# A transformer block with its backward pass on one core: a centred start, a reordered W2 stage, later h1 stores and one reordered FFN pair

## Chip, cores, metric

One core of one Trainium2 chip. The metric is the device time of one execution in microseconds (us), lower is better.

## The reference

Forward and backward of one block: layernorm, linear attention with 32 heads of 20, layernorm, gated FFN. x is 2048 x 640, the FFN is 1728 wide, all in bf16. What the change touches is the forward half:

```python
def _A_ref(x, wqkv, wo):                     # x is already layernormed
    q, k, v = ...                            # x @ wqkv, 32 heads
    phi = lambda t: jnp.where(t > 0, t + 1, jnp.exp(t)) + 1e-6
    pq, pk = phi(q), phi(k)
    kv = jnp.einsum("bhsd,bhse->bhde", pk, v)
    z = jnp.einsum("bhsd->bhd", pk)
    ...                                      # (pq kv) / (pq z) @ wo
h  = x + _A_ref(_layernorm(x), wqkv, wo)
h2 = h + _B_ref(_layernorm(h), w_gate, w_up, w_down)     # (silu(g) * u) @ w_down
# returned: h2 and the gradients for x and the five weights
```

## The kernel before

Sixteen token tiles of 128 rows. In the start, each tile is normalised on VectorE, transposed on TensorE (`ps_t`), copied by ScalarE (`xnT`) and multiplied with the k and q weights (`ps_kq`); exp and relu are ScalarE's, the rest of phi VectorE's.

```python
    def ln1(t):
        nc.vector.tensor_scalar(out=xn[:, t, :], in0=x_tm[...], scalar1=mv1[:, t, 0:1],
                                scalar2=rstd1[:, t:t + 1], op0=ALU.subtract, op1=ALU.mult)
        ...  # 5 transposes into ps_t, nc.scalar.copy into xnT
    # ... (cut)
        warm(42); ln1_stats(0); ln1(0); warm(10)
        act = kq_mm(0, 0); ln1(1); act()
        ln1_stats(2); kq_mm(1, 0)(); kq_mm(0, 1)()
        for t in range(1, ST):
            if t + 1 < ST: ln1(t + 1)
            if t == 2: kq_phi(0)
            if t > 1: kq_mm(t, 0)()
            if t + 2 < ST: ln1_stats(t + 2)
            # ... (cut)
            kq_mm(t, 1)()
            if t > 1: kq_phi(t - 1)
```

Then come z, Y = xn^T pk (`ps_y`), KV, and the W2 stage. `dm(1)` is an independent piece of FFN backward, ten products and a ScalarE copy, used as filler.

```python
        for t in range(0, 12, 4):
            normalise(t)                       # VectorE, about 8.3 us
            if t < 8: tr_pqs(t)                # four DMA transposes on SP
        for t in range(3): load_xr(t)
        # ... KV products and their VectorE masks (cut)
        dm(1)
        for i in range(DT):
            ps = mm("ps_w2t")
            mm_heads(ps, ...)
            nc.scalar.copy(out=half(W2T[:, i, :]), in_=row(ps))
            nc.sync.dma_start_transpose(out=W2[...], in_=W2T[:, i, :])
        tr_pqs(8); normalise(12); tr_pqs(12)
        dm(4)
        for t in range(ST + 2):
            if t < ST:
                xr = xrs.pop(t)
                ps = mm("ps_a"); mm_row(ps, ...)                       # pqsT x W2
                nc.vector.tensor_tensor(out=half(xr[:]), in0=row(ps), in1=half(xr[:]), op=ALU.add)
                nc.scalar.dma_start(out=scr_h1_v[:, t, :], in_=xr[:])  # the h1 store
                # ... statistics (cut)
                dm(1)
            if t > 0: load_xr(t + 2)
            u = t - 2
            # ... hn(u) on VectorE, its transpose on SP (cut)
```

Four FFN groups follow (`pg`, `pu`, seven VectorE multiplications and sums a tile pair, then `ps_dw`, the weight gradient), and from `ps_dhn` on the backward of attention, which the change touches in one VectorE line (`tk`).

The names in short: pqs is pq divided by its normaliser; ps_a is the output of attention, xr are the rows of x to which it is added, and the sum is h1; hn is h1 normalised; pg and pu are the gate and up products of the FFN. A name with ps_ is a tile in PSUM, where TensorE's products land; the program uses these buffers in turn, so a product may have to wait until the copy out of its buffer has ended. "Before" and "after" are the first two traces.

Of the kernel before, what the change touches and what calls it, by code (L numbers as in the profile page):

```python
# [10 lines left out]
ALU = mybir.AluOpType  # L11
# [4 lines left out]
P = 128  # L16
# [4 lines left out]
def kernel(  # L21
# [8 lines left out]
    nc = tc.nc  # L30
# [36 lines left out]
    def row(ps):  # L67
        return ps[:, :, :320]
# [35 lines left out]

    def mm_row(ps, lhs, rhs, n, start=True, stop=True, by_k=False):

        steps = [(ci, k) for ci in range(2) for k in range(n)]
        if by_k:
            steps.sort(key=lambda x: x[1])
        for ci, k in steps:  # L110
            nc.tensor.matmul(ps[:, ci, :320], lhsT=lhs(k), rhs=rhs(k, *NCH[ci]),  # L111
                             start=(start and k == 0), stop=(stop and k == n - 1))

# [84 lines left out]

    nc.sync.dma_start(out=x_tm[0][:, 0, 0:320], in_=x_v[:, 0, 0:320])
    nc.scalar.dma_start(out=x_tm[0][:, 0, 320:640], in_=x_v[:, 0, 320:640])  # L200
    load_x(nc.scalar, 1, 2)
    w_k = A_wqkv[:, D:2 * D].rearrange("(k p) n -> p k n", p=P)
    nc.sync.dma_start(out=wqk[:, 0:3, D:2 * D], in_=w_k[:, 0:3, :])
    nc.sync.dma_start(out=wqk[:, 3:5, D:2 * D], in_=w_k[:, 3:5, :])
# [6 lines left out]
    def load_2():  # L211
        yield load_x(nc.sync, 2, 3)
        yield nc.sync.dma_start(out=wqk[:, :, 0:D], in_=A_wqkv[:, 0:D].rearrange("(k p) n -> p k n", p=P))
        yield load_x(nc.sync, 3, 4)

    def load_3():
# [43 lines left out]
    ers = {}  # L260

    def ln1_stats(t):
        st = ln_stats(x_tm[t // 8][:, t % 8, :], mv1[:, t, :])
        if t == 0:
            wait_for(st, load_2())
        ln_rstd(mv1[:, t:t + 1, :], rstd1, t, 1, nc.vector if t < 2 else nc.gpsimd)

    def ln1(t):
        nc.vector.tensor_scalar(out=xn[:, t, :], in0=x_tm[t // 8][:, t % 8, :], scalar1=mv1[:, t, 0:1],
                                scalar2=rstd1[:, t:t + 1], op0=ALU.subtract, op1=ALU.mult)  # L270
        tp = psum.tile([P, D], BF16, name="ps_t", tag="mm")
        for kt in range(DT):
            nc.tensor.transpose(tp[:, kt * P:(kt + 1) * P], xn[:, t, kt * P:(kt + 1) * P], ident[:])
        tpv = tp[:].rearrange("p (k c) -> p k c", c=P)
        if t == 0:
            ln1_stats(1)
            wait_for(nc.scalar.copy(out=xnT[:, t, 0:3], in_=tpv[:, 0:3]), load_3())
            nc.scalar.copy(out=xnT[:, t, 3:5], in_=tpv[:, 3:5])
        else:
            nc.scalar.copy(out=xnT[:, t], in_=tpv)  # L280

    def kq_mm(t, which):
        dst, w0 = ((pk, D), (pqa, 0))[which]
        ps = mm("ps_kq")
        mm_row(ps, lambda k: xnT[:, t, k, :], lambda k, n0, n1: wqk[:, k, w0 + n0:w0 + n1], DT, by_k=(t == 0))

        def act():
            e = fw("phi_e")
            r = fw("phi_r")
            nc.scalar.activation(out=e[:, :, :320], in_=row(ps), func=ACT.Exp)  # L290
            nc.scalar.activation(out=r[:, :, :320], in_=row(ps), func=ACT.Relu)
            ers.setdefault(t, []).append((dst, e, r))

        return act
# [14 lines left out]
    with tc.manual_schedule(engines={EngineType.PE, EngineType.DVE, EngineType.Activation}):  # L309
# [6 lines left out]

        warm(42)
        ln1_stats(0)
        ln1(0)
        warm(10)  # L320
        act = kq_mm(0, 0)
        ln1(1)
        act()
        ln1_stats(2)
        kq_mm(1, 0)()
        kq_mm(0, 1)()
        for t in range(1, ST):
            if t + 1 < ST:
                ln1(t + 1)
            if t == 2:  # L330
                kq_phi(0)
            if t > 1:
                kq_mm(t, 0)()
            if t + 2 < ST:
                ln1_stats(t + 2)
            if t == 1:
                kq_phi(0, last=False)
            kq_mm(t, 1)()
            if t > 1:
                kq_phi(t - 1)  # L340
        kq_phi(ST - 1)

# [91 lines left out]
    with tc.manual_schedule(engines={EngineType.PE, EngineType.DVE, EngineType.SP}):  # L434
# [15 lines left out]
        dm(1)  # L450
        for t in range(0, 12, 4):
            normalise(t)
            if t < 8:
                tr_pqs(t)
        for t in range(3):
# [15 lines left out]
        dm(1)  # L471
        for i in range(DT):
            ps = mm("ps_w2t")
            mm_heads(ps, lambda j: wo6[:, j, i * P:(i + 1) * P], lambda j, a, b: KVT[:, j, a:b])
            nc.scalar.copy(out=half(W2T[:, i, :]), in_=row(ps))
            nc.sync.dma_start_transpose(out=W2[:, :, i * P:(i + 1) * P], in_=W2T[:, i, :])
        tr_pqs(8)
        normalise(12)
        tr_pqs(12)
        dm(4)  # L480

# [3 lines left out]
        for t in range(ST + 2):  # L485
            if t < ST:
# [3 lines left out]
                nc.vector.tensor_tensor(out=half(xr[:]), in0=row(ps), in1=half(xr[:]), op=ALU.add)  # L490
                nc.scalar.dma_start(out=scr_h1_v[:, t, :], in_=xr[:])
                mv = small.tile([P, 4, 2], FP32, name="mv2", tag="mv2")
# [11 lines left out]
            if u == 2:  # L504
                nc.sync.dma_start(out=mat_v(scr_W2T), in_=W2T)
            h1, mv = h1s.pop(u)
            nc.vector.tensor_scalar(out=hn[:, u, :], in0=h1[:], scalar1=mv[:, 0, 0:1],
                                    scalar2=rstd2[:, u:u + 1], op0=ALU.subtract, op1=ALU.mult)
# [3 lines left out]
    with tc.manual_schedule(engines={EngineType.SP}):  # L512
# [13 lines left out]
        for g in range(4):  # L526
# [4 lines left out]
            for t in range(0, ST, 2):  # L531
# [27 lines left out]
                nc.scalar.copy(out=u, in_=pu[:, :, :w])  # L559
                a = fw("a")[:, :, :w]  # L560

                nc.vector.tensor_tensor(out=m, in0=m, in1=dg, op=ALU.mult)  # L562
                nc.vector.tensor_tensor(out=a, in0=u, in1=dmv, op=ALU.mult)
                nc.vector.tensor_tensor(out=nsg, in0=nsg, in1=m, op=ALU.mult)
                nc.vector.tensor_tensor(out=du, in0=m, in1=dmv, op=ALU.mult)
                nc.vector.tensor_tensor(out=nsg, in0=nsg, in1=dg, op=ALU.add)
                nc.vector.tensor_tensor(out=m, in0=m, in1=u, op=ALU.mult)  # L567
                nc.vector.tensor_tensor(out=dg, in0=a, in1=nsg, op=ALU.mult)
                for c in range(2):
# [146 lines left out]
    with tc.manual_schedule(engines={EngineType.SP, EngineType.DVE}):  # L716
# [65 lines left out]
        WK2 = wvk[:, 1]  # L782
        for i in range(DT):
            ps = mm("ps_wk2")
            mm_heads(ps, lambda j: wqkvT[:, 10 + j, i * P:(i + 1) * P], lambda j, a, b: dKVT[:, j, a:b])
            nc.scalar.copy(out=half(WK2[:, i, :]), in_=row(ps))
            nc.sync.dma_start_transpose(out=WV2[:, :, i * P:(i + 1) * P], in_=WK2[:, i, :])
        ps = mm("ps_dzb")
        mm_row(ps, lambda k: ones[:], lambda k, n0, n1: dzE[k][:, n0:n1], 2)
# [29 lines left out]
        for t in range(ST + LAG):  # L819
            if t in (2, 3):  # L820
                dwqk(0, t + 1, t + 2)
            if t < ST:
# [6 lines left out]
                mm_row(ps, lambda i: xnT_r[:, t, i, :], lambda i, n0, n1: WK2[:, i, n0:n1], DT)  # L829
                nc.vector.tensor_tensor(out=half(tk[:]), in0=row(ps), in1=half(dzb[:]), op=ALU.add)  # L830
                nc.vector.tensor_tensor(out=dk[:, t, :], in0=tk[:], in1=pkr[:], op=ALU.mult)
# [118 lines left out]
```

## Time and profile before

| kernel before | us |
|---|---|
| median of the first runs (823.25 to 825.19) | 823.6 |
| the profiled one of these | 825.2 |
| TensorE busy in it | 815.3 of a span of 823.3 |

The prediction below shows the waits and the chain. A line of the timeline gives start, duration, engine, line, operation, tile, sizes, count; in brackets idle time before and what ended it. Kernel before, W2 stage:

```profile
91.45 2.20 PE L130 MATMUL ps_w2t<-yk,wvo 128*128 128x120 bf16 x35
...
91.65 0.91 ACT L377 CAST dm<-ps_dm 128x896 bf16<-128x896 f32 x1 [2.79 <-PE ps_dm L363]
92.45 3.09 ACT L475 CAST wvo<-ps_w2t 128x640 bf16<-128x640 f32 x5
...
93.80 2.43 PE L363 MATMUL ps_dm<-wdT,dh2T 128*128 128x448 bf16 x12
```

Thirty-five small products take TensorE from 91.45 to 93.80, 2.35 us for five tiles. ScalarE needs 0.91 and 3.09 us for the copies that empty those PSUM tiles, one after the other. TensorE is shown busy, yet its starts show that it is held to ScalarE's pace: the products of the fourth tile start at 92.61 and those of the fifth at 93.20, each right after a copy has ended (92.55 and 93.15).

### The profile page before, as it was taken

Reading aid. Unit: us, or ns where it says so; the run is one execution under the profiler, and the core shown is the slowest. Engines: PE = TensorE matmul, PEld = TensorE weight load, DVE = VectorE, ACT = ScalarE, POOL = GpSimd, SP = SyncE. Lnnn points to the kernel's source line nnn. Section 1 sums busy time; section 2 is a strip of 40 time slices with the busy share of each in tenths; the row PEclk is TensorE's granted clock in tenths of the full one; section 3 lists DMA queues with packets and bytes.
Section 4 is the critical chain, followed back from the end, with each engine's and each line's share of the span. In section 5 each row is a group of like instructions: output and inputs, shape, how many; then the busy total and the mean of one; then the engine's idle time right before and its main releaser. Section 6 shows DMA issues by size and latency. Waiting matters only on the chain.

```text
span 823.3 us, 14095 instructions
## 1 busy us (share of the span) xinstructions
PE 815.3 (99%) x5549; PEld 522.8 (63%) x5549; DVE 444.0 (54%) x875; ACT 291.3 (35%) x412; POOL 187.2 (23%) x343
## 2 busy tenths in 40 slices
PE   8999999999999999999999999999999999999998
PEld 6766656555555555555556677777776777777776
DVE  6978767791077018810660147787884366632222
ACT  6982422670084125500741122322322133322101
POOL 2330022322312231221126301211220112112330
PEclk9999999999999999999999999999999999999999
DMA  9993589999658898893498937978599989899942
GB/s 300 191 355 88 137 190 262 284 231 201 163 104 202 190 215 204 195 264 86 99 252 185 286 72 218 232 195 175 115 241 160 177 147 183 170 191 266 268 135 73
DMA packets 278369, 158.53 MB, mean 193 GB/s; under 512 B 235036, under 2 KB 264925, under 8 KB 278304
## 3 DMA queue, kind: packets, MB, share of 16 engines
q1 hardware_dynamic: 251600, 81.96, 53.6%
q0 software_dynamic: 17744, 64.45, 25.1%
q10 hardware_dynamic: 8960, 11.24, 4.2%
q8 instruction: 43, 0.70, 0.4%
q14 instruction: 22, 0.18, 0.1%
HBM read 47.60 MB, written 53.66 MB: 123 GB/s over the span
## 4 chain that ended last, share of the span: by engine, by line
PE 85%; DVE 8%; DMA 3%; ACT 1%; SPq 1%; issue 1%; POOL 0%; ACTq 0%; DVEq 0%
PE ps_dw L607 20%; PE ps_dhn L111 14%; PE ps_dxn L852 8%; PE ps_o L907 7%; PE ps_dwqk L111 5%; PE ps_kq L111 4%; PE pg L535 4%; PE pu L540 4%; PE ps_dm L363 3%; PE ps_y L111 3%; PE ps_dk L111 3%; PE ps_gt L658 3%; PE ps_dp L111 3%; PE pdm L363 2%; DMA xr<-in_A_x_dram 1%; DVE m_s L562 1%
## 5 line engine op out<-in xcount | busy, mean ns | idle before, releaser
L111 PE MATMUL ps_dhn<-wgT,cols 128*128 128x320 bf16 x864 | 119.5, 299 | 0.0
L607 PE MATMUL ps_dw<-dd,hn 128*128 128x448 bf16 (+1 forms) x640 | 118.8, 346 | 0.0
L111 PEld LDWEIGHTS <-cols 128*128 128x128 bf16 x864 | 84.5, 98 | 32.9
L607 PEld LDWEIGHTS <-hn 128*128 128x128 bf16 x640 | 62.6, 98 | 54.2
L609 DVE CAST dwev<-ps_dw 128x896 bf16<-128x896 f32 (+3 forms) x12 | 10.9, 908 | 124.0 <-PE ps_dw L607 124.0
L609 ACT CAST dwev<-ps_dw 128x896 bf16<-128x896 f32 (+1 forms) x20 | 17.6, 878 | 158.5 <-PE ps_dw L607 158.5
L572 POOL DMA_DIRECT2D scr_dT<-stg x64 | 34.7, 542 | 168.4 <-DMA stg<-dd 162.2
L149 DVE CUSTOM_DVE_ANT_0 lb_a<-lb_dy,hn 128x640 bf16<-128x640 bf16 x32 | 26.4, 826 | 75.4 <-ACT lb_dy L147 75.4
L540 PE MATMUL pu<-wgu,hnT 128*128 128x448 bf16 (+1 forms) x320 | 63.6, 346 | 0.0
L535 PE MATMUL pg<-wgu,hnT 128*128 128x448 bf16 (+1 forms) x320 | 63.6, 346 | 0.0
L907 PE MATMUL ps_o<-wd,mT 128*128 128x320 bf16 (+2 forms) x462 | 62.8, 295 | 0.0
L607 PE MATMUL ps_dw<-m_s,dh 128*128 128x448 bf16 (+1 forms) x320 | 60.7, 346 | 0.6 <-DVE m_s L567 0.6
L852 PEld LDWEIGHTS <-ring 128*128 128x128 bf16 x480 | 46.9, 98 | 18.3
L907 PEld LDWEIGHTS <-mT 128*128 128x128 bf16 x462 | 44.0, 98 | 16.2 <-issue 0.3
L852 PE MATMUL ps_dxn<-wqkvT,ring 128*128 128x320 bf16 x320 | 51.3, 299 | 0.0
L607 PEld LDWEIGHTS <-dh 128*128 128x128 bf16 x320 | 31.3, 98 | 28.0 <-issue 1.1
L540 PEld LDWEIGHTS <-hnT 128*128 128x128 bf16 x320 | 31.3, 98 | 27.1
L535 PEld LDWEIGHTS <-hnT 128*128 128x128 bf16 x320 | 31.3, 98 | 27.1
L363 PEld LDWEIGHTS <-dh2T 128*128 128x128 bf16 x320 | 31.2, 98 | 26.6 <-issue 1.5
L363 PE MATMUL ps_dm<-wdT,dh2T 128*128 128x448 bf16 (+1 forms) x240 | 46.7, 344 | 1.2 <-ACT dm L377 1.0
L111 PE MATMUL ps_kq<-wqk,xnT 128*128 128x320 bf16 x320 | 46.1, 300 | 0.9 <-ACT xnT L280 0.8
L147 ACT ACTIVATE lb_dy<-ps_dhn,rstd 128x640 bf16<-128x640 f32 x16 | 12.7, 793 | 87.6 <-PE ps_dhn L111 87.6
(160 smaller groups left out, 1276.4 us busy)
## 6 DMA issues: line engine op xcount, KB each, us to landing
scr_dT<-stg POOLq DMA_DIRECT2D x48, 224.0 KB, 3.1
cols<-scr_dT POOLq DMA_DIRECT2D x6, 1728.0 KB, 8.4
scr_m<-m_s POOLq DMA_DIRECT2D x12, 448.0 KB, 4.4
cols<-scr_dT ACTq DMA_DIRECT2D x2, 1728.0 KB, 8.3
out_dram<-dwev POOLq DMA_DIRECT2D x30, 112.0 KB, 2.2
scr_dT<-stg POOLq DMA_DIRECT2D x16, 192.0 KB, 2.6
scr_pk<-pk SPq DMA_DIRECT2D x4, 640.0 KB, 7.6
scr_pq<-pqa SPq DMA_DIRECT2D x4, 640.0 KB, 7.9
```

The source lines that it names most:

```text
L111: nc.tensor.matmul(ps[:, ci, :320], lhsT=lhs(k), rhs=rhs(k, *NCH[ci]), start=(start and k == 0), stop=(stop and k == n - 1))
L147: nc.scalar.activation(out=half(dy[:]), in_=row(ps), func=ACT.Copy, scale=rstd_col, accum_out=sums[:, 0:1])
L149: nc.vector.tensor_tensor_reduce(out=a[:], in0=dy[:], in1=xhat, scale=1.0, scalar=0.0, op0=ALU.mult, op1=ALU.add, accum_out=sums[:, 1:2])
L363: nc.tensor.matmul(ps[:, c, :w], lhsT=dh2T[:, kt, (t + c) * P:(t + c + 1) * P], rhs=wdT[:, kt, o:o + w], start=(kt == 0), stop=(kt == DT - 1))
L535: nc.tensor.matmul(pg[:, c, :w], lhsT=hnT[:, kt, (t + c) * P:(t + c + 1) * P], rhs=wg[:, kt, 0:w], start=(kt == 0), stop=(kt == DT - 1))
L540: nc.tensor.matmul(pu[:, c, :w], lhsT=hnT[:, kt, (t + c) * P:(t + c + 1) * P], rhs=wg[:, kt, w:2 * w], start=(kt == 0), stop=(kt == DT - 1))
L572: nc.gpsimd.dma_start(out=scr_dT[t + c, :, KO[g]:KO[g] + GK[g], :], in_=stg[:, :GK[g], :])
L607: nc.tensor.matmul(ps[:, c, :w], lhsT=lhs(t), rhs=rhs(t), start=(t == 0), stop=(t == ST - 1))
L609: copy(out=ev[:, :len(parts), :w], in_=ps[:, :len(parts), :w])
L658: nc.tensor.matmul(ps[:, ci, :320], lhsT=dh1[:, t, i * P:(i + 1) * P], rhs=pqs_tm[:, t, n0:n1], start=(t == 0), stop=(t == ST - 1))
L852: nc.tensor.matmul(ps[:, ci, :320], lhsT=lhs[:, i, :], rhs=rhs[:, i, n0:n1], start=(k == 0 and i == 0), stop=(k == 2 and i == DT - 1))
L907: nc.tensor.matmul(po, lhsT=mT[:, t % 4, j, :], rhs=wd[:, j, n0:n1], start=(j == 0), stop=(j == FT - 1))
```

## The change

It means to fill TensorE's last idle pieces: tiles 0 and 1 are only centred (the scale 1/std is applied in exp and relu), so that GpSimd's power is not on the way to the first transposes; the transposes of the next tile go between k and q products; a dm block goes into the W2 stage and one normalisation behind it; h1 is stored two tiles later; in the last tile pair of each FFN group one multiplication moves behind those that `ps_dw` waits for.

```diff
-    nc.sync.dma_start(out=x_tm[0][:, 0, 0:320], in_=x_v[:, 0, 0:320])
-    nc.scalar.dma_start(out=x_tm[0][:, 0, 320:640], in_=x_v[:, 0, 320:640])
+    load_x(nc.sync, 0, 1)
...                                  (q weights as two transfers, not one)
+        if t < NC:                                             # NC = 2
+            nc.vector.tensor_scalar(out=xn[:, t, :], in0=..., scalar1=mv1[:, t, 0:1],
+                                    scalar2=None, op0=ALU.subtract)
+        else:
+            ln1_xn(t)
...
+            sc = rstd1[:, t:t + 1] if t < NC else 1.0
-            nc.scalar.activation(out=e[:, :, :320], in_=row(ps), func=ACT.Exp)
+            nc.scalar.activation(out=e[:, :, :320], in_=row(ps), func=ACT.Exp, scale=sc)
...                                  (relu alike)
-        warm(42)
+        warm(31)
...
-        warm(10)
+        warm(12)
...
+                kq_mm(t, 0, (lambda: ln1(t + 1)) if t + 1 < ST else None)()
...
+            if t >= ST - NC:
+                ln1_xn(t - ST + NC)
...
-        for t in range(0, 12, 4):
+        for t in (0, 4):
             normalise(t)
-            if t < 8:
-                tr_pqs(t)
+            tr_pqs(t)
...
         for i in range(DT):
+            if i == 3:
+                dm(1)
             ps = mm("ps_w2t")
...
-        tr_pqs(8)
-        normalise(12)
-        tr_pqs(12)
-        dm(4)
+        for t in (8, 12):
+            normalise(t)
+            tr_pqs(t)
+        dm(3)
...
-                nc.scalar.dma_start(out=scr_h1_v[:, t, :], in_=xr[:])
...
+            nc.scalar.dma_start(out=scr_h1_v[:, u, :], in_=h1[:])
...
+                for o in ((0, 1, 2, 3, 4, 5, 6) if t < ST - 2 else (0, 2, 3, 4, 5, 1, 6)):
+                    nc.vector.tensor_tensor(out=ops[o][0], in0=ops[o][1], in1=ops[o][2], op=ops[o][3])
...
-                nc.vector.tensor_tensor(out=half(tk[:]), in0=row(ps), in1=half(dzb[:]), op=ALU.add)
+                nc.vector.scalar_tensor_tensor(out=half(tk[:]), in0=row(ps), scalar=rstd1[:, t:t + 1] if t < NC else 1.0,
+                                               in1=half(dzb[:]), op0=ALU.mult, op1=ALU.add)
```

More of the change, by code (lines that the diff above doesn't have):

```diff
@@ L103, in bc, with mm_row @@
         return ap.unsqueeze(2).to_broadcast([P, H, Dh])
-    def mm_row(ps, lhs, rhs, n, start=True, stop=True, by_k=False):
-        steps = [(ci, k) for ci in range(2) for k in range(n)]
-        if by_k:
-            steps.sort(key=lambda x: x[1])
-        for ci, k in steps:
-            nc.tensor.matmul(ps[:, ci, :320], lhsT=lhs(k), rhs=rhs(k, *NCH[ci]),
-                             start=(start and k == 0), stop=(stop and k == n - 1))
+    def mm_row(ps, lhs, rhs, n, start=True, stop=True):
+        for ci in range(2):
+            for k in range(n):
+                nc.tensor.matmul(ps[:, ci, :320], lhsT=lhs(k), rhs=rhs(k, *NCH[ci]),
+                                 start=(start and k == 0), stop=(stop and k == n - 1))
     OH = [120 * j for j in range(5)] + [D - P]
@@ L197, in load_x @@
         return eng.dma_start(out=x_tm[t0 // 8][:, t0 % 8:(t1 - 1) % 8 + 1, :], in_=x_v[:, t0:t1, :])
-    nc.sync.dma_start(out=x_tm[0][:, 0, 0:320], in_=x_v[:, 0, 0:320])
-    nc.scalar.dma_start(out=x_tm[0][:, 0, 320:640], in_=x_v[:, 0, 320:640])
+    load_x(nc.sync, 0, 1)
     load_x(nc.scalar, 1, 2)
     w_k = A_wqkv[:, D:2 * D].rearrange("(k p) n -> p k n", p=P)
+    w_q = A_wqkv[:, 0:D].rearrange("(k p) n -> p k n", p=P)
     nc.sync.dma_start(out=wqk[:, 0:3, D:2 * D], in_=w_k[:, 0:3, :])
@@ L212, in load_2 @@
         yield load_x(nc.sync, 2, 3)
-        yield nc.sync.dma_start(out=wqk[:, :, 0:D], in_=A_wqkv[:, 0:D].rearrange("(k p) n -> p k n", p=P))
+        yield nc.sync.dma_start(out=wqk[:, 0:3, 0:D], in_=w_q[:, 0:3, :])
         yield load_x(nc.sync, 3, 4)
+        yield nc.sync.dma_start(out=wqk[:, 3:5, 0:D], in_=w_q[:, 3:5, :])
     def load_3():
@@ L260 @@
     ers = {}
+    NC = 2
     def ln1_stats(t):
@@ L265, in ln1_stats, with ln1_xn, ln1_rstd, ln1 @@
             wait_for(st, load_2())
-        ln_rstd(mv1[:, t:t + 1, :], rstd1, t, 1, nc.vector if t < 2 else nc.gpsimd)
-    def ln1(t):
+    def ln1_xn(t):
         nc.vector.tensor_scalar(out=xn[:, t, :], in0=x_tm[t // 8][:, t % 8, :], scalar1=mv1[:, t, 0:1],
                                 scalar2=rstd1[:, t:t + 1], op0=ALU.subtract, op1=ALU.mult)
+    def ln1_rstd(t):
+        ln_rstd(mv1[:, t:t + 1, :], rstd1, t, 1)
+    def ln1(t):
+        if t < NC:
+            nc.vector.tensor_scalar(out=xn[:, t, :], in0=x_tm[t // 8][:, t % 8, :], scalar1=mv1[:, t, 0:1],
+                                    scalar2=None, op0=ALU.subtract)
+        else:
+            ln1_xn(t)
         tp = psum.tile([P, D], BF16, name="ps_t", tag="mm")
@@ L275, in ln1 @@
         if t == 0:
-            ln1_stats(1)
             wait_for(nc.scalar.copy(out=xnT[:, t, 0:3], in_=tpv[:, 0:3]), load_3())
@@ L280, in ln1, with kq_mm @@
             nc.scalar.copy(out=xnT[:, t], in_=tpv)
-    def kq_mm(t, which):
+    def kq_mm(t, which, between=None):
         dst, w0 = ((pk, D), (pqa, 0))[which]
         ps = mm("ps_kq")
-        mm_row(ps, lambda k: xnT[:, t, k, :], lambda k, n0, n1: wqk[:, k, w0 + n0:w0 + n1], DT, by_k=(t == 0))
+        for k0, k1 in ((0, 3), (3, DT)) if t == 0 else ((0, DT),):
+            for ci, (n0, n1) in enumerate(NCH):
+                for k in range(k0, k1):
+                    nc.tensor.matmul(ps[:, ci, :320], lhsT=xnT[:, t, k, :], rhs=wqk[:, k, w0 + n0:w0 + n1],
+                                     start=(k == 0), stop=(k == DT - 1))
+            if between and (t > 0 or k0 == 0):
+                between()
         def act():
@@ L289, in act @@
             r = fw("phi_r")
-            nc.scalar.activation(out=e[:, :, :320], in_=row(ps), func=ACT.Exp)
-            nc.scalar.activation(out=r[:, :, :320], in_=row(ps), func=ACT.Relu)
+            sc = rstd1[:, t:t + 1] if t < NC else 1.0
+            nc.scalar.activation(out=e[:, :, :320], in_=row(ps), func=ACT.Exp, scale=sc)
+            nc.scalar.activation(out=r[:, :, :320], in_=row(ps), func=ACT.Relu, scale=sc)
             ers.setdefault(t, []).append((dst, e, r))
@@ L315, in warm @@
                 nc.tensor.matmul(ps[:, 0, :P], lhsT=ident[:], rhs=ident[:], start=True, stop=True)
-        warm(42)
+        warm(31)
         ln1_stats(0)
+        ln1_rstd(0)
         ln1(0)
-        warm(10)
-        act = kq_mm(0, 0)
-        ln1(1)
-        act()
+        warm(12)
+        ln1_stats(1)
+        ln1_rstd(1)
+        kq_mm(0, 0, lambda: ln1(1))()
         ln1_stats(2)
+        ln1_rstd(2)
         kq_mm(1, 0)()
@@ L327 @@
         for t in range(1, ST):
-            if t + 1 < ST:
-                ln1(t + 1)
+            if t == 1:
+                ln1(2)
+            if t > 1:
+                kq_mm(t, 0, (lambda: ln1(t + 1)) if t + 1 < ST else None)()
             if t == 2:
                 kq_phi(0)
-            if t > 1:
-                kq_mm(t, 0)()
             if t + 2 < ST:
                 ln1_stats(t + 2)
+                ln1_rstd(t + 2)
             if t == 1:
@@ L560 @@
                 a = fw("a")[:, :, :w]
-                nc.vector.tensor_tensor(out=m, in0=m, in1=dg, op=ALU.mult)
-                nc.vector.tensor_tensor(out=a, in0=u, in1=dmv, op=ALU.mult)
-                nc.vector.tensor_tensor(out=nsg, in0=nsg, in1=m, op=ALU.mult)
-                nc.vector.tensor_tensor(out=du, in0=m, in1=dmv, op=ALU.mult)
-                nc.vector.tensor_tensor(out=nsg, in0=nsg, in1=dg, op=ALU.add)
-                nc.vector.tensor_tensor(out=m, in0=m, in1=u, op=ALU.mult)
-                nc.vector.tensor_tensor(out=dg, in0=a, in1=nsg, op=ALU.mult)
+                ops = [(m, m, dg, ALU.mult), (a, u, dmv, ALU.mult), (nsg, nsg, m, ALU.mult), (du, m, dmv, ALU.mult),
+                       (nsg, nsg, dg, ALU.add), (m, m, u, ALU.mult), (dg, a, nsg, ALU.mult)]
+                for o in ((0, 1, 2, 3, 4, 5, 6) if t < ST - 2 else (0, 2, 3, 4, 5, 1, 6)):
+                    nc.vector.tensor_tensor(out=ops[o][0], in0=ops[o][1], in1=ops[o][2], op=ops[o][3])
                 for c in range(2):
@@ L782, with wk2 @@
         WK2 = wvk[:, 1]
-        for i in range(DT):
+        def wk2(i):
             ps = mm("ps_wk2")
@@ L787 @@
             nc.sync.dma_start_transpose(out=WV2[:, :, i * P:(i + 1) * P], in_=WK2[:, i, :])
+        for i in range(DT):
+            wk2(i)
         ps = mm("ps_dzb")
```

## The prediction

> **What bounds the kernel now.** I read the page first: busy times, then the chain that ended last.
>
> ```profile
> PE 815.3 (99%) x5549; PEld 522.8 (63%) x5549; DVE 444.0 (54%) x875; ACT 291.3 (35%) x412; POOL 187.2 (23%) x343
> ...
> PE 85%; DVE 8%; DMA 3%; ACT 1%; SPq 1%; issue 1%; POOL 0%; ACTq 0%; DVEq 0%
> ```
>
> TensorE is busy for 815.3 of 823.3 us and is 85% of the chain. The change takes no product away, except 9 warm-up products (42+10 become 31+12). So it can win at most the 8.0 us in which TensorE idles. Of these 1.4 lie before its first instruction and 2.9 after its last product (a start of 820.4 in the timeline, to the end at 823.3), and the change touches neither. Some 3.7 are left. The list of waits, read for PE alone, says where:
>
> ```profile
> PE ps_warm L315 <- POOL ident masks.py:199: 1.4, 1, 1.4
> PE ps_dm L363 <- ACT dm L377: 1.0, 1, 1.0
> PE ps_kq L111 <- ACT xnT L280: 0.8, 1, 0.8
> PE ps_dw L607 <- DVE m_s L567: 0.6, 2, 0.3
> ```
>
> The long waits of ACT, DVE and POOL in that list (158 us and less) are engines waiting for TensorE and cost nothing. The change aims at the last three lines: 0.8 and some small pieces at the start, 1.0 where dm alternates with ps_a, 0.6 at the two ends of FFN groups. Next, the timeline of the start:
>
> ```profile
> 3.10 0.89 DVE L136 BATCH_NORM_STATS2 st<-x_tm 128x6 f32<-128x320 bf16 x2 [1.73 <-DMA x_tm<-in_A_x_dram]
> ...
> 4.50 0.57 POOL L142 TENSOR_TENSOR rstd<-lnv,nhalf 128x1 f32<-128x1 f32 x1 [3.14 <-DVE lnv L141]
> ...
> 5.12 0.45 DVE L269 TENSOR_SCALAR xn<-x_tm,mv,rstd 128x640 bf16<-128x640 bf16 x1 [0.69 <-POOL rstd L142]
> ...
> 9.08 0.71 ACT L290 ACTIVATE phi_e<-ps_kq 128x640 bf16<-128x640 f32 x1
> ...
> 13.35 0.70 ACT L280 COPY xnT<-ps_t 128x640 bf16<-128x640 bf16 x1
> ...
> 14.10 2.89 PE L111 MATMUL ps_kq<-wqk,xnT 128*128 128x320 bf16 x20
> ...
> 17.23 0.45 PE L273 MATMUL ps_t<-ident,xn 128*128 128x128 bf16 x5 [0.24 <-DVE xn L269]
> ...
> 20.24 0.45 PE L273 MATMUL ps_t<-ident,xn 128*128 128x128 bf16 x5
> ```
>
> The first normalised tile waits for GpSimd. But from 9.08 on ScalarE runs six activations, then the copy of tile 2 (13.35), and TensorE takes tile 2 at 14.10: there ScalarE leads. From 17.23 the period is 3.01 us a tile, and VectorE, busy without a gap in the same stretch, has that period too. Last, the chain in order of time around the ps_a loop:
>
> ```profile
> 104.58 4.42 DMA pqsT<-pqa
> ...
> 109.09 0.34 ACTq L491 DMA_DIRECT2D scr_h<-xr  x1
> ...
> 110.43 2.05 PE ps_dm L363 x10
> ...
> 146.33 5.01 DMA xr<-in_A_x_dram
> ...
> 152.67 1.28 ACT L556
> ...
> 186.02 0.55 DVE m_s L567
> 186.61 5.46 PE ps_dw L607 x28
> ```
>
> The first store of h1 waits until a transpose of pqs has landed (109.0), though its data were there at 103.7; in the compiled program it waits on a completion semaphore that this transpose used before it. ScalarE stands behind it, its copy of dm is late, TensorE idles 1.05 us. Further on the chain leaves TensorE: loads of xr, stores of h1, then VectorE without a gap from 156.5 to 186.6, and TensorE waits 0.34 for the last m_s.
>
> **What the Trainium skill says.**
> 1. "TensorE: Matmul & The Clock Gate", section "What's actually happening": the array runs at half rate until a window of about 3.4 us has been busy; the window runs free. The trace agrees: of the 42 warm-up products the first 33 start 107 ns apart, and from 4.95 us on, 3.5 us after the first, they start 56 ns apart.
> 2. "ScalarE: Activation LUTs", section "What ACT_TABLE_LOAD costs": each per-partition pointer operand (a scale, say) adds about 93 ns to an activation. The trace agrees: 640 columns from PSUM take 691 ns as the copy dp, 793 ns as lb_dy, which has a pointer scale.
> 3. "DMA: Bandwidth & Descriptors", section "Issuing engines are not separate DMA queues": transfers from different engines share the same 16 DMA engines. So x of tile 0 as one transfer of 160 KB in place of two halves doesn't come sooner. In the trace the two halves of 80 KB took 2.3 and 2.5 us.
> 4. "VectorE: DVE Perf Modes", section "The perf-mode tier table": a two-tensor operation with a PSUM operand runs at 1x. The trace's tk (640 columns, PSUM) takes 819 ns, against 492 for such sums from SBUF. Whether the scaled form is the same is not shown; I take 0.82.
>
> **The change, part by part.**
>
> *Start.* Removed before the first transposes: add 0.15 and power 0.57 with their hand-overs, 5.12 - 4.25 = 0.87 us. Against it, tile 0 lands as one transfer, shared with tile 1: estimate +0.2 (twice the bytes ahead at the observed ramp). So the first transposes come at about 4.95 and not 5.62. This doesn't reach the end of the stretch, because exp and relu of tile 0 now need rstd, and the compiled order of GpSimd is three adds and then three powers. The third add needs the statistics of tile 2. Its load was issued at 4.26, when the statistics of tile 0 were done; the median of the loads of tiles 2 and 3 is 4.1 and tile 3 took 5.4, so tile 2 took 2.8 and lands at 7.05, later by the same 0.2: 7.25. Statistics 0.9 + 0.2, add and hand-over 0.35, power 0.57: 9.3. Exp of tile 0 thus starts at 9.3, before 9.08. Then six activations at 0.60 apart plus 0.09 for the pointer: 6 x 0.69 = 4.15. Copy of tile 2 at 13.45 for 0.70, products at 14.2, before 14.10. The weights of q, split in two, land last at about 10.5 and make TensorE wait within this stretch, hidden behind ScalarE. What is really won: the transposes of the next tile lie between k and q, so xn is needed 1.36 us later, and the wait at 17.23 (0.4) goes. Before, tile 3 and the transposes of tile 4 are done at 20.24 (17.23 + 3.01). After: tile 3's transposes are not yet done at 14.2, so 14.2 + 2 x 3.01 = 20.22. Start: 0.0, from -0.4 to +0.6 (the latter if the pointer doesn't slow the pace and x is not later).
>
> *W2 and dm, h1 stores.* The interleaving removes the 0.15 before the dm block at 93.80. The compiled ScalarE order puts only the first two stores of h1 one dm copy later; the rest is in the same order as before. That suffices for the 1.05: the copy in question runs before the store. TensorE is 1.2 earlier at ps_a, but the chain then isn't TensorE's. VectorE now masks KVT ahead of the third normalisation (8.4 each), so the fourth ends near 106.8 and not 98.4. The last four transposes on SP start at 106.9, before 105.97; the latter took 2.3 in place of 1.3, so the end of that queue is at 112.1, before 112.3. From there come xr of tile 3, the SP and DMA chain and VectorE's FFN work: 0.2 won.
>
> *Last FFN pair.* One multiplication, at a pace of 0.53, moves behind m. At group 0: 0.53 + 0.2 = 0.7 won, of the 0.34 + 1.2 that TensorE could use; it will wait about 0.8 there. I take 0.6, since part of the loop may not follow. At group 3 the wait is 0.26 and goes whole: 0.26.
>
> *Others.* The two extra normalisations, 2 x 0.44 on VectorE near 53 us, fall where statistics have ended: 0. The scaled tk: 16 x 0.82 as before, with no TensorE wait behind it: 0.
>
> Sum: 0.0 + 0.6 + 0.26 = 0.9; I add 0.1 for small hand-overs: 823.83 - 1.0 = 822.8.
>
> **Rivals.**
> *The start gains its full 0.7 or more.* For: VectorE and GpSimd lose 0.87 at the head, and the 0.8 wait of ps_kq belongs to that. Against: ScalarE's chain from 9.08. It would make 822.1, with 1.2 in the loop 821.5.
> *New waits eat all.* The late fourth normalisation could hold back the last pqs transposes with the 2.3 us issue still there (+0.8), or two of the later stores; against: ps_a of these tiles is only needed after 140. It would make 823.6 to 824.2.
> *The clock rises a window later*, since 31 warm-ups end at 4.74 (1.42 + 31 x 0.107) and TensorE then idles 0.2. For: the window runs free. Against: that window is 94% busy. Tile 0 at half rate would cost 1.5: 824.3.
> *All of the 3.7 us is won*: 820.1. Against: no part touches all waits.
>
> **Range and chances.** 822.8, with 821.3 at the good end of the first rival and 824.1 where a new wait or clock eats all; three runs of before spread over 1.8 us. A gain over 2% would be 16.5 us, twice all of TensorE's idle time: 0.005. A loss of 2% would need a stage that stops feeding TensorE: 0.01.
>
> **What would show it.** First transposes near 4.9 to 5.0; exp of tile 0 no earlier than 9.1, released by GpSimd; copy of tile 2 within 0.3 of 13.45; no wait for xn in the steady stretch. No 1.0 wait of ps_dm for ScalarE. The wait of ps_dw for m_s at group 0 remains, and grows to 0.5 to 1.0; that of group 3 is gone. tk at 0.8 to 0.9. I am wrong if TensorE reaches the z products over 0.6 earlier than at 56.23, or if that wait at group 0 is gone, or if warm-ups are still 107 ns apart after 5.3.

## The result and the profile after

The changed kernel took 822.9 us (median of 4 runs, 822.44 to 823.39) against 823.6: ratio 0.9988, 95% interval 0.9970 to 1.0005. A ratio is the mean time of one kernel's fast runs over that of the other's fast runs of the same rounds, so it is not quite the ratio of the medians quoted. In later rounds on another chip it was 0.9978 (0.9966 to 0.9990). It is within 2% and, by those second rounds, a little faster. All outputs are right.

The profile after is of a run of 822.7 us, so the two traces differ by 2.5 us and the timed medians by 0.7. What TensorE waits for now (in total, times, longest):

```profile
PE ps_warm L332 <- POOL ident masks.py:199: 1.4, 1, 1.4
PE ps_kq L298 <- ACT xnT L290: 1.0, 2, 0.8
PE ps_t L284 <- DVE xn L278: 0.7, 1, 0.7
PE ps_dm L385 <- ACT dmst L399: 0.2, 1, 0.2
PE ps_wk L128 <- ACT wvk L807: 0.2, 1, 0.2
PE ps_z L370 <- DVE pk L319: 0.2, 1, 0.2
```

The waits of 1.0 (`ps_dm`), 0.6 (`ps_dw`) and 0.2 (`ps_kvt`) are gone; that of `ps_kq` is still there; that of `ps_t` (0.24 at 17.23 before) now stands at the first transposes; new ones stand at `ps_z` and, behind another copy, at `ps_dm`. Timeline of the start after:

```profile
3.96 0.89 DVE L134 BATCH_NORM_STATS2 st<-x_tm 128x6 f32<-128x320 bf16 x2 [2.59 <-DMA x_tm<-in_A_x_dram]
...
5.57 0.71 PE L284 MATMUL ps_t<-ident,xn 128*128 128x128 bf16 x5 [0.67 <-DVE xn L278]
...
8.78 1.62 POOL L140 TENSOR_TENSOR rstd<-lnv,nhalf 128x1 f32<-128x1 f32 x3
8.95 2.89 PE L298 MATMUL ps_kq<-wqk,xnT 128*128 128x320 bf16 x20 [0.24 <-ACT xnT L290]
9.39 0.79 ACT L307 ACTIVATE phi_e<-ps_kq,rstd 128x640 bf16<-128x640 f32 x1 [0.50 <-POOL rstd L140]
...
13.46 0.73 ACT L290 COPY xnT<-ps_t 128x640 bf16<-128x640 bf16 x1
...
14.25 0.45 PE L298 MATMUL ps_kq<-wqk,xnT 128*128 128x320 bf16 x2 [0.77 <-ACT xnT L290]
```

x of tile 0 lands at 3.96 (3.10 before), so the first transposes come at 5.57, hardly before the old 5.62, and at half rate (0.71 for five). The k products of tile 1 come 0.28 earlier (8.95, before 9.23), but ScalarE's copy of tile 2 comes at 13.46 (13.35 before), and the lead is gone. The W2 stage after:

```profile
91.25 1.05 PE L128 MATMUL ps_w2t<-yk,wvo 128*128 128x120 bf16 x21
...
92.25 1.89 ACT L498 CAST wvo<-ps_w2t 128x640 bf16<-128x640 f32 x3
92.40 2.05 PE L385 MATMUL ps_dm<-wdT,dh2T 128*128 128x448 bf16 x10
...
94.29 0.75 PE L128 MATMUL ps_w2t<-yk,wvo 128*128 128x120 bf16 x14
```

The five tiles now take TensorE 1.15 + 0.60 (from 91.25 to 92.40, from 94.29 to 94.89) and not 2.35: 0.60 won, where the prediction had 0.15. The idle time in the list of waits did not show it, because the ends of the products are modelled; the starts show it. (The stage wins 0.26 more at `ps_kvt`, see below.) This is what the Trainium skill says in "Perfetto Trace Analysis", section "Tensor Engine Instruction (MATMUL, LD_WEIGHTS)": the profiler estimates the end time of TensorE's instructions. Last, the chain of the ps_a loop after, in order of time:

```profile
111.48 1.28 SPq L447
...
112.80 2.88 DMA xr<-in_A_x_dram
...
115.77 0.84 DVE xr L513
...
127.83 5.59 DMA xr<-in_A_x_dram
...
133.54 0.84 DVE xr L513
...
135.85 0.29 ACTq L529
...
136.18 0.81 ACT dmst L399
...
137.03 1.79 PE ps_dm L385 x10
```

The last pqs transposes on SP hold back the load of xr of tile 3, so VectorE runs late; a later load, of tile 9, takes 5.59 us (the median is 3.3) and makes it late again; the store of h1 on ScalarE stands behind VectorE's hn, the copy of dm behind the store, and TensorE waits 0.23 at 137.03. (The second trace of the changed kernel has 0.47 there.)

**One table for all traces.** Each trace was cut where TensorE starts a stage, and the lengths compared (us, from the starts of TensorE's products). "start" is the time of the first ps_y; "W2" is ps_y to ps_a; "loop" ps_a to pg; "group 0" from the first pg of group 0 to that of group 1; "group 3" from its first pg to ps_dhn. Groups 1 and 2 took 166.47 and all after ps_dhn 364.66 to 364.68 in every one, so nothing happens there. The names are those of the experiments below.

| trace | start | W2 | loop | group 0 | group 3 | end |
|---|---|---|---|---|---|---|
| before | 57.62 | 43.74 | 49.18 | 76.17 | 65.42 | 823.27 |
| before again (b_again) | 58.38 | 43.74 | 47.97 | 75.67 | 65.41 | 822.31 |
| b_late | 57.92 | 43.74 | 47.98 | 75.67 | 65.42 | 821.87 |
| b_head | 57.69 | 43.74 | 47.97 | 75.86 | 65.42 | 821.83 |
| b_ffn | 57.43 | 43.74 | 48.84 | 76.18 | 65.00 | 822.32 |
| b_inter | 57.40 | 42.88 | 47.97 | 76.36 | 65.41 | 821.16 |
| b_body | 57.61 | 42.88 | 48.25 | 76.24 | 65.00 | 821.11 |
| after | 57.68 | 42.88 | 48.40 | 75.67 | 65.00 | 820.76 |
| after again (a_again) | 57.58 | 42.88 | 48.72 | 75.67 | 65.00 | 820.98 |
| a_pool | 57.59 | 42.88 | 48.56 | 75.67 | 65.00 | 820.85 |
| a_warm | 57.40 | 42.88 | 48.68 | 75.67 | 65.00 | 820.75 |
| a_xr | 57.58 | 42.88 | 48.16 | 75.67 | 65.00 | 820.42 |
| a_start | 58.71 | 43.10 | 49.80 | 76.55 | 65.00 | 824.29 |
| a_both | 59.52 | 43.10 | 48.00 | 75.67 | 65.00 | 822.42 |

W2 and group 3 are fixed by the program: 0.86 and 0.42 won wherever the change is in. (a_start and a_both have 43.10: another 0.22 goes into their first ps_y products, which wait for the second of the two late normalisations.) Start, loop and group 0 vary between executions of one kernel. For the two traces first compared the difference of 2.51 is -0.06 (start) + 0.86 + 0.78 (loop) + 0.50 (group 0) + 0.42; for the second pair (b_again, a_again), of 1.33, it is 0.80 + 0.86 - 0.75 + 0.00 + 0.41. The same change, and the variable terms even change sign.

### The profile page after: what moved, and what is told of

The parts are those of the page before. It is cut to its first block, busy times and chain, and to the rows that moved or that the text cites. A ratio compares the mean times of both kernels' runs of the same rounds, so it can differ in the third digit from the quotient of the medians.

```text
span 820.8 us, 14051 instructions
## 1 busy us (share of the span) xinstructions
PE 814.0 (99%) x5540; PEld 523.4 (64%) x5540; DVE 443.8 (54%) x875; ACT 291.5 (36%) x412; POOL 187.4 (23%) x345
## 4 chain that ended last, share of the span: by engine, by line
PE 87%; DVE 6%; ACT 3%; DMA 2%; issue 1%; SPq 1%; POOL 0%; DVEq 0%; ACTq 0%
PE ps_dw L627 21%; PE ps_dhn L109 14%; PE ps_dxn L877 8%; PE ps_o L932 7%; PE pu L563 7%; PE pg L558 7%; PE ps_dwqk L109 5%; PE ps_y L109 3%; PE ps_dp L109 3%; PE ps_dk L109 3%; PE ps_gt L678 3%; PE pdm L385 2%; PE ps_dm L385 2%; DVE st L134 1%; ACT phi_r L308 1%; DMA xr<-in_A_x_dram 1%
## 5 line engine op out<-in xcount | busy, mean ns | idle before, releaser
L109 PE MATMUL ps_dhn<-wgT,cols 128*128 128x320 bf16 x864 | 119.5, 299 | 0.0
L109 PEld LDWEIGHTS <-cols 128*128 128x128 bf16 x864 | 84.5, 98 | 32.9
```

The source lines that it names most:

```text
L109: nc.tensor.matmul(ps[:, ci, :320], lhsT=lhs(k), rhs=rhs(k, *NCH[ci]), start=(start and k == 0), stop=(stop and k == n - 1))
```

## Experiments

Each call has its own runs of the kernel before, on its own chip: medians 825.02, 824.95 and 825.24 us. Compare ratios, not the medians.

**b_again: the kernel before, once more.** No edit.

> The kernel before once more, unaltered, for a second trace and more times. The two traces on record differ by 2.5 us in span (823.3 and 820.8), the medians of the timed runs only by 0.7. Theory: the trace of before on record caught one of its slow runs (825.2 against a median of 823.6), and its extra 1.5 us lie between the W2 products and the first pg (91 to 150 us), where the chain runs over transfers. Then this trace shows the z products at 56.2 (within 0.1), pg near 149.0 to 149.5 in place of 150.5, and ends near 821.5 to 822. Rival: the extra lies in the start (landing of x, clock): z products near 55. Rival 2: it lies in the FFN groups (ps_dw of group 0 at 180.8, dhn at 458.6 minus 1.5).

824.43 us (823.18 to 825.68), ratio 0.9995. The trace (a run of 824.28) is not that of the first:

```profile
PE ps_kq L111 <- ACT xnT L280: 0.8, 1, 0.8
PE ps_t L273 <- DVE xn L269: 0.6, 1, 0.6
PE ps_dw L607 <- DVE m_s L567: 0.3, 1, 0.3
```

The wait of ps_dm (1.0) is not there, nor that of ps_dw at group 0; the start is 0.76 later, with a wait of 0.6 for xn. So the theory was half right: the first trace did have extras in the loop (1.21) that are not in every run. But none of its three figures came: this run had extra time in the start, the z products at 56.99 and not 56.2, pg at 150.10 and the end at 822.31. The first store of h1 shows the loop's part. Here, on ScalarE:

```profile
107.65 0.35 ACTq L491 DMA_DIRECT2D scr_h<-xr  x1
108.04 0.91 ACT L377 CAST dm<-ps_dm 128x896 bf16<-128x896 f32 x1 [4.80 <-DVE xr L490]
```

In the first trace it was issued at 109.09 (the chain in the prediction). 1.4 us earlier, and the copy behind it holds nobody up.

**a_again: the changed kernel, once more.** No edit.

> The changed kernel once more, unaltered. Theory: 0.7 to 1.0 us faster than the kernel before (822.4 to 823.1); ps_dw of group 0 has no wait for m_s, pg near 149.0. In its trace on record x of tile 0 landed at 3.96 and the clock rose at 6.4. If both belong to the change they come back: landing after 3.7, warm-ups 107 ns apart to after 6.2. If they were chance, landing near 3.1 to 3.4, and the z products come up to 0.7 earlier than 56.0.

823.28 us (822.75 to 823.59), ratio 0.9978: a gain of about 1.8 us, twice what was expected here. x landed at 3.60, the clock rose near 7.0, and z came at 55.92. The later landing belongs to the change: x of tile 0 lands between 3.52 and 3.96 in all eight traces that load it as one transfer, and between 3.04 and 3.12 in the six with two halves. The time of the clock's rise does not: it is near 4.3 in a_pool. The kernel varies less than the one before: 0.84 us between its 5 runs, where the 11 runs of before of these rounds span 3.07 (823.14 to 826.21).

**b_head: the start alone** (the parts of the diff down to the late ln1_xn, and tk; W2, stores and FFN as before).

> Only the start of the change (centred tiles, transposes between k and q, x of tile 0 whole, q weights in two, 31 and 12 warm-ups, scaled tk); W2, stores and FFN pairs as before. Theory, as predicted: 0.0 (within 0.3) against before, 823.4 to 823.9. Rival (start gains its full 0.7): 822.9. Rival (late clock and late x cost more than they show): 824.3.

823.79 us, ratio 0.9989 (0.9976 to 1.0002). Five of six runs lie between 823.41 and 823.84, one at 826.16. In the trace the start is 57.69. By the traces the start wins nothing over a good run of before, as predicted; by the times this is not shown, for the interval reaches from 0.24% faster to 0.02% slower, and the ratio is as low as those of b_inter and b_ffn below. Over the six traces with the old start (57.40 to 58.38, mean 57.73) the six with this start or nearly so (b_head, the two of the changed kernel, a_pool, a_warm, a_xr: 57.40 to 57.69, mean 57.59) vary less.

**b_body: all but the start.**

> All of the change but the start. Theory: the whole gain of the change is here, 822.6 to 823.0 (ratio about 0.999). If the start costs something that the two traces hide (late clock), this is faster than the changed kernel: 821.2 to 822, as the traces' difference of 2.4 us from 60 us on says. Rival: the parts need each other, 823.4 or more.

823.11 us (822.40 to 823.51), ratio 0.9976 (0.9964 to 0.9988), not to be told from the changed kernel's 0.9978. Within these intervals the whole gain of the change is in its body.

**b_inter: the W2 stage alone** (the loop over `(0, 4)` as in the diff above).

```diff
         for i in range(DT):
+            if i == 3:
+                dm(1)
...
-        tr_pqs(8); normalise(12); tr_pqs(12); dm(4)
+        for t in (8, 12): normalise(t); tr_pqs(t)
+        dm(3)
```

> The kernel before with only the new order of W2 and dm (dm between the third and fourth W2 product, the third normalisation after W2). Its compiled ScalarE order is that of the changed kernel: the copy of dm stands ahead of the first h1 store. Theory after the first six traces: the W2 block loses 1.17 us of stretched spacing before and 0.34 after, so ps_a comes 0.8 earlier after ps_y; the long wait of ps_dm for ScalarE near 110 cannot come; a new wait of 0.3 to 0.6 near 136 gives part back; the waits of ps_dw at groups 0 and 3 stay (0.5 or less, and 0.39). Time 0.2 to 0.8 below the kernel before of the same rounds, and a narrower spread. As predicted it would be 0.15 in the W2 block.

823.83 us (823.10 to 824.63), ratio 0.9987 (0.9973 to 1.0001); its runs span 1.5, those of before 2.9. The gain of about 1.1 us is a little above the 0.2 to 0.8 expected. W2 takes 42.88. No wait in the loop at all in this trace, so the expected 0.3 to 0.6 near 136 was missed; but at the ends of the groups:

```profile
PE ps_dw L608 <- DVE m_s L568: 0.8, 2, 0.5
```

**b_late: the h1 store alone.**

```diff
-                nc.scalar.dma_start(out=scr_h1_v[:, t, :], in_=xr[:])
...
+            nc.scalar.dma_start(out=scr_h1_v[:, u, :], in_=h1[:])
```

> The kernel before with only the store of h1 written two tiles later. The compiled ScalarE order stays that of before (and the same completion semaphores), so the theory says: no change (ratio 0.999 to 1.001), the wide spread of before stays (over 1.5 us between its runs). Rival, as the change intends: the wait for the transpose of pqs goes with it, then the spread narrows and the time falls by 0.5 to 1.2.

825.15 us (823.78 to 826.73), ratio 1.0002. Nothing, and the wide spread stays. ScalarE's order is the scheduler's in this stretch, and the compiled order of copies and stores on ScalarE is that of before, store for store. It is the new order of b_inter that puts one more copy ahead of the first store in the compiled program; the later store in the source does nothing by itself. Which of b_inter's two moves does it, the dm block or the third normalisation (with which VectorE's first sum comes 5.9 us after the first ps_a and not 1.6), was not separated.

**b_ffn: the last FFN pair alone** (the reordered operations of the diff).

> The kernel before with only the last FFN pair of each group reordered. Theory: 0.39 won at group 3 in every run, group 0 between 0 and 0.5, so 0.4 to 0.9 below before; spread as before. From the first ps_dw of group 3 to the first dhn 39.00 in place of 39.42.

824.07 us (823.07 to 825.10), ratio 0.9988 (0.9974 to 1.0001). Group 3 takes 65.00 in place of 65.42, as expected; group 0 gained nothing in this trace (76.18). And the wait of the loop is back, in a second trace:

```profile
PE ps_dm L363 <- ACT dm L377: 0.7, 1, 0.7
```

So of five traces with the old W2 stage two have it (1.21 and 0.87 of stretched spacing), three do not; of nine with the new one none has it near 110.

**a_xr: x rows five tiles ahead, on top of the change.**

```diff
-        for t in range(3):
+        for t in range(5):
             load_xr(t)
...
-            if t > 0:
-                load_xr(t + 2)
...
             nc.sync.dma_start_transpose(out=hnT[...], in_=hn[:, u, :])
+            load_xr(u + 5)
```

> The changed kernel with the x rows of the ps_a loop loaded five tiles ahead (tiles 3 and 4 up front), not three. If the lag of VectorE in that loop comes from the load of tile 3 that stands behind the pqs transposes on SP (issued at 112.8, landed 115.7), VectorE's sum of tile 3 comes before 112, the wait of ps_dm near 136 (0.23 and 0.47 in the two traces) is gone, and the time falls by 0.2 to 0.5 against the changed kernel. Rival: VectorE is late because its fourth normalisation ends at 106.5; then the wait stays and the time is the same.

822.26 us (821.96 to 822.51, six runs), ratio 0.9966 (0.9953 to 0.9978): the lowest ratio and the narrowest spread. The changed kernel's 0.9978 is from other rounds, so the step of some 0.0012 (1.0 us) between them is an estimate and their intervals overlap; the trace agrees in kind, ending 0.33 to 0.56 before those of the changed kernel, a_pool and a_warm. VectorE's sums of tile 3, which came at 115.77 (before 112 was expected), and of tile 10:

```profile
112.33 0.82 DVE L513 TENSOR_TENSOR xr<-ps_a,xr 128x640 bf16<-128x640 f32 x1
...
136.24 0.82 DVE L513 TENSOR_TENSOR xr<-ps_a,xr 128x640 bf16<-128x640 f32 x1 [3.02 <-DMA xr<-in_A_x_dram]
```

The first follows tile 0's hn without idle time. Of the later ones seven wait for ps_a (5.2 us in all) and only three still for memory (3.9; in the trace after six did, 9.9). No wait of ps_dm is left, and the loop takes 48.16; the 0.18 to 0.19 above the best lies inside the first ps_a. The rival (VectorE late because its fourth normalisation ends at 106.5) falls: the first sum is at 106.36 here too, and the wait is gone all the same. Not separated: all loads came two tiles earlier, so it is not shown how much is the load of tile 3 and how much the longer lead of the later ones. What goes with the wait is VectorE's sum of tile 9. In the five traces with the wait (after, a_again, a_pool, a_warm, a_start) it comes 32.9 to 34.4 us after the first ps_a; in the four with the new order and no wait there (b_inter, b_body, a_xr, a_both) 30.3 to 32.4.

**a_pool: GpSimd in program order** (`EngineType.Pool` added to the engines of the manual schedule of the start; power of tile 0 ahead of the sum of tile 2).

> The changed kernel with GpSimd in program order alone. Theory: the power of tile 0 ends before 6.5 and exp of tile 0 starts when ScalarE has copied tile 1 (8.9 to 9.1) in place of 9.39 and 8.98, so between 0 and 0.4 of the wait of ps_kq goes; time within 0.3 of the changed kernel. Rival, as predicted: the order of GpSimd (three sums, then three powers) is the reason why the start gains nothing; then z comes by 55.4.

822.91 us, ratio 0.9971 (0.9959 to 0.9984), the trace's start 57.59 and end 820.85: the same as the changed kernel's. In the timeline of its start:

```profile
8.60 0.79 ACT L307 ACTIVATE phi_e<-ps_kq,rstd 128x640 bf16<-128x640 f32 x1
...
10.37 0.79 ACT L307 ACTIVATE phi_e<-ps_kq,rstd 128x640 bf16<-128x640 f32 x1 [0.29 <-PE ps_kq L298]
...
12.05 0.79 ACT L307 ACTIVATE phi_e<-ps_kq,rstd 128x640 bf16<-128x640 f32 x1 [0.20 <-PE ps_kq L298]
...
13.41 0.69 ACT L290 COPY xnT<-ps_t 128x640 bf16<-128x640 bf16 x1
...
14.16 0.72 PE L298 MATMUL ps_kq<-wqk,xnT 128*128 128x320 bf16 x4 [0.52 <-ACT xnT L290]
```

Exp of tile 0 comes 0.8 earlier (8.60; 8.9 to 9.1 was expected) and the copy of tile 2 at 13.41, as without the edit. ScalarE waits for the k products of tile 1 (10.37) and for the q products of tile 0 (12.05), and then has the scaled activations and the copy. The second wait belongs to this run: the q weights held TensorE for 0.22 there. Without it the copy would come about 0.2 earlier (estimate).

**a_warm: 42 and 10 warm-up products again.**

> The changed kernel with 42 and 10 warm-up products, as before the change. Theory: the clock rises again near 4.95 (warm-ups from there 56 ns apart), the transposes of tile 0 take 0.45 in place of 0.71, but ScalarE sets the end of the start, so z stays at 55.9 to 56.1 and the time within 0.2 of the changed kernel. Rival: the late clock costs the difference between the 4.95 expected and the 5.2 to 5.6 seen: 0.3 to 0.6 faster.

822.74 us, ratio 0.9972 (0.9959 to 0.9984): the same. The clock rose at 5.3, the five transposes took 0.44, and ps_kq still waited 0.78 for the copy of tile 2. No effect of the number of warm-ups on the time is shown.

**a_start: another start on top of the change.** GpSimd in program order; xn, transposes and copy of tile 2 ahead of q of tile 0; relu of k of tile 1 on VectorE; the late ln1_xn after the last phi.

```diff
+            if t == 1 and which == 0:
+                ln1(2)
+                nc.vector.tensor_scalar(out=r[:, :, :320], in0=row(ps), scalar1=sc, scalar2=0.0,
+                                        op0=ALU.mult, op1=ALU.max)
+            else:
                 nc.scalar.activation(out=r[:, :, :320], in_=row(ps), func=ACT.Relu, scale=sc)
...
-            if t >= ST - NC:
-                ln1_xn(t - ST + NC)
         kq_phi(ST - 1)
+        for t in range(NC):
+            ln1_xn(t)
```

> The changed kernel with another start: GpSimd in program order (power of tile 0 before the sum of tile 2), xn, transposes and copy of tile 2 ahead of the q products of tile 0, the relu of k of tile 1 on VectorE, the two late normalisations after the last phi. Theory: ScalarE, full from the exp of tile 0 on, is why the start gained nothing. Then exp of tile 0 starts at 8.9 to 9.1, the wait of ps_kq for the copy of tile 2 (0.77 and 0.59) is gone, and the z products come at 55.0 to 55.4 in place of 55.9 to 56.0. In the loop of ps_a most of it is given back (wait near 136 grows to about 1), so 0.0 to 0.5 below the changed kernel. Rival: x and weights from memory set the pace of the start; then z stays at 55.8 or later.

824.83 us, ratio 0.9994 (0.9980 to 1.0007): worse than a_pool and a_warm of the same rounds. Its waits:

```profile
PE ps_dm L388 <- ACT dmst L402: 1.0, 1, 1.0
PE ps_t L284 <- DVE xn L270: 0.9, 2, 0.6
PE ps_y L109 <- DVE xn L270: 0.7, 1, 0.7
```

The wait for the copy of tile 2 is gone, as intended, and the transposes of tile 3 come at 14.46 in place of 15.62. But VectorE, with 0.88 more to do there, gives xn of tile 4 late (0.61 at 18.24), and from then on the transposes come every 3.01 to 3.02 us (once 3.43), where the changed kernel has 3.00; the late normalisations hold ps_y by 0.7. So z came at 56.26 and not at 55.0 to 55.4. ScalarE is not alone at the limit: from 20 to 50 us of the trace after, TensorE and ScalarE are both shown busy for 30.0 of 30.0 us and VectorE for 27.3. This kernel changed several things at once and two of them were bad choices; it doesn't show what the copy of tile 2 moved by itself would bring. That stays open.

**a_both: a_start with the loads of a_xr.**

> The start of the run before and the x rows five tiles ahead. Theory: both gains add, since the loop no longer gives anything back: 0.5 to 1.0 below the changed kernel with the loads alone, 1.3 to 2 below the changed kernel, about 821.4 to 821.8 where that has 822.3. Rival: VectorE's FFN work of group 0 takes it back (a wait of ps_dw for m_s over 0.4).

824.19 us, ratio 0.9986: the gains do not add, since one of them was none. It does confirm a_xr: with the start 1.8 us later than the changed kernel's, the loop takes 48.00 and has no wait, where a_start had 49.80 with a wait of 1.0.

## Why the prediction was right, and where it was not

The total was right: 822.8 told, 822.9 measured. The gain was told as 1.0 us; it was 0.7 between the first medians and about 1.8 by the ratio of the later rounds, so the close agreement is in part luck. Step by step:

- **What bounds the kernel, and that little can be won:** right. The fixed gains are 1.28 us. But the gaps shown are no strict limit: the W2 products gave 0.60 where 0.15 of idle time was shown.
- **Start, 0.0:** right in size (the first ps_y is 0.06 later in the first pair), wrong in the reason. First transposes at 4.95: wrong, 5.57 and 5.21, since x as one transfer landed 0.86 and 0.50 later, where the step had 0.2, and this eats the 0.87 saved. Exp of tile 0 at 9.3: 9.39 and 8.98. Copy of tile 2 at 13.45: 13.46 and 13.39. GpSimd's compiled order does hold exp back in the trace after (0.50, by rstd), and the copy follows 4.07 behind it (4.15 told). But a_pool shows that it is worth little: with exp 0.8 earlier, ScalarE waits for products of TensorE instead, and at most about 0.2 is left open. The other half of the step, the activations with a pointer, held: between the exp of k of tile 1 and the copy of tile 2 stand four of them, 0.67 to 0.70 apart and not 0.60, about 0.3 us more (estimate). That is as much as the 0.28 by which the k products of tile 1 start earlier. The step also misread two lines: ScalarE's six activations from 9.08 are not one run, for it waits 0.42 at 10.80 for the k products of tile 1, and the wait at 17.23 is 0.24 and not 0.4. (The clock rose at 5.01 in that trace, not at 4.95.) Nor do the z products, 0.22 earlier after, win anything: the second half of them waits for pk of the last tile, which follows ScalarE's last relu (56.33, before 56.27).
- **W2 stage, 0.15:** the term that was mis-sized. It is 0.86. The step took the idle time of the list of waits; TensorE was held to ScalarE's copies, and modelled ends hid most of it (0.60). The other 0.26 is at ps_kvt, whose 30 products take 1.55 and not 1.81: VectorE's masks of KV no longer stand behind the third normalisation and start at 88.27 and not 88.61. The list of before puts the wait of 0.2 there down to a copy of dm that ended at 88.86; after, that copy ends at 88.92 and nobody waits for it.
- **The wait of 1.05 in front of the h1 stores, removed by the compiled order:** the wait is gone, and the compiled order is as told, one copy of dm ahead of the first two stores. The step did not say which edit makes this order: b_late shows that the later store does not, b_inter has it. And it was a wait of two of five traces, not of the kernel: taking it from one trace and the time from a median of others mixed two things.
- **"The chain is not TensorE's, 0.2 net":** right that a part is given back, wrong where. It is not at the FFN: pg came 1.58 earlier and stayed so. It is in the loop itself: in four traces (after, a_again, a_pool, a_warm) the loop takes 0.43 to 0.75 more than the loop without waits (47.97). Of this 0.31 to 0.63 lies at the wait near 137, behind late loads of xr; a_xr moves the loads ahead and that wait goes with it. The rest, 0.04 to 0.40, lies inside the first ps_a, where a_warm's list names the transpose of W2 (`PE ps_a L109 <- DMA wvo<-wvo: 0.2, 1, 0.2`): TensorE now comes to it earlier. The step had named that queue end (112.1 told, 112.75 seen), but carried it to the wrong place.
- **Group 0, a wait that remains and grows to 0.5 to 1.0:** wrong as a forecast for the changed kernel. Its two traces, a_pool and a_warm have none. Yet b_again and b_late, with the old order of the FFN pair, have none at that place either, and b_body, with the new one, has 0.57. It goes with how late VectorE comes out of the loop: in the five traces that lose 0.5 or more in group 0 its last sum of the loop starts 0.8 to 1.5 us after the first pg, in the other nine 0.2 to 0.6. What makes it late in one run and not in another is not settled. **Group 3, 0.26:** it is 0.42 by the spacing, in every trace.
- **The scaled tk:** right. 818 ns with a constant, as before; 880 ns for the two with a pointer.
- **The late clock as a rival:** two of the three signs that I had called proof against me came true, this and group 0. The cost forecast for it (1.5) did not come: with this start and rises between 5.3 and 7.0, z lies between 55.73 and 56.03 (a_warm, a_xr, the two of the changed kernel, b_head). The rise itself varies between runs of one start, so it is no mark of the change.

So the number was right partly because errors met. In its sum W2, loop and group 0 are one term of 0.6; the first pair of traces has 0.86 + 0.78 + 0.50 = 2.14 for it and the second 0.86 - 0.75 + 0.00 = 0.11. 0.87 was too little for W2 and group 3, against new waits in the loop and gains counted from a slow trace. The fixed part is shown by the table. That the spread of before (1.9 to 3.1 us in the four sets of rounds) shrinks to about 1 us is measured (on 4 and 5 runs against 4 to 11); that the missing waits at 110 are the main cause fits the traces but was not counted run by run.

## What to carry to other kernels

Before working from the waits of one profile, compare the profiled run's time with the median, and take a second profile: a wait that is in one trace of two is not a term of the sum. Measure a stage by the starts of its first and of the next stage's first product; idle time between TensorE instructions shows only part of what a slow reader of PSUM costs (here 0.15 of 0.60). And read the compiled order before crediting a source line: here the new order of the W2 stage, not the moved store, changed who stands behind whom. And loads moved ahead of a queue of transposes took away a wait that the moved store, the number of warm-ups and the new start left in place.

## What the Trainium skill lacked or had wrong

- "TensorE: Matmul & The Clock Gate", "What's actually happening": it says that the transition point varies by 500 ns up or down. With the same start code and 42 warm-ups, the first of them at 1.42 us in both, the full rate came at 4.25 us in one trace (b_ffn) and at 6.92 in another (b_late), 2.67 us apart.
- "Perfetto Trace Analysis", "Tensor Engine Instruction (MATMUL, LD_WEIGHTS)": it says that TensorE's ends are estimated, but that section doesn't say what to do about it. Idle time showed 0.15 behind the W2 products, where the spacing of starts then gave 0.60.
- "VectorE: DVE Perf Modes", "The perf-mode tier table": no row for a scalar_tensor_tensor. With one operand of 640 columns from PSUM it took 818 ns with a constant, the same as a tensor_tensor, and 880 ns with a pointer.
- "DMA: Bandwidth & Descriptors": no duration for the issue of a DMA transpose of this size, SBUF to SBUF, on SP. For one tile of 128 x 640 SP was busy 1.28 us, at times 2.3, and a plain load behind eight of them in SP's order was issued only when the last was done (112.80).
